# Two reorderings in a packed-attention and mixer kernel: bank by bank out of the fold, and a step ahead of w2's conversion

## The chip, the cores and the metric

The kernel runs on one core of one Trainium2 chip. The metric is the device time of one execution in microseconds (us); lower is better. The kernel before the change takes 829.05 us, the median of three runs (829.01 to 829.96 us).

The core's engines appear in the profile as PE (TensorE matmuls) and PEld (its weight loads), DVE (VectorE), ACT (ScalarE), POOL (GpSimd) and SP (SyncE, which here only issues DMAs). Each engine works through its own instructions in order and waits for the others at semaphores.

## What is computed

For eight batches, eight heads, 576 tokens and a head width of 64, with 32 packed rows `p` for each head:

```python
p_packed = softmax(scale * p @ k.T) @ v            # 32 rows for each head
out      = softmax(scale * q @ p_packed.T) @ p_packed
x  = out, heads side by side                       # 576 x 512 for each batch
u  = x + (x.T @ U @ V).T                           # rank 32 along the tokens
ch = relu(u @ w_ch1) @ w_ch2                       # 512 -> 2048 -> 512
result = u + ch
```

`U`, `V`, `w_ch1` and `w_ch2` arrive as 64-bit floats. The kernel takes them apart with integer operations on DVE ("conversion").

## The kernel before, in words

**Numbers.** Where more than one pass of precision is wanted a matrix is held as a high part and a low part; the product is then three matmuls (`mm3`, lines 85 to 89). A split is always the same pair: ACT copies the source into the high part with rounding, then DVE subtracts that from the source to get the low part.

**The fold.** The output of the second attention is never multiplied by `w_ch1` directly. For each batch `b` and each quarter `c` of `w_ch1`'s 2048 columns, `fold(b, c)` (lines 379 to 392) multiplies the packed rows of the eight heads by their part of `w_ch1`: sixteen small matmuls into two PSUM banks, `f_ps[0]` for heads 0 to 3 and `f_ps[1]` for heads 4 to 7. Each bank has 512 columns. They are emptied by four splits of 256 columns: an ACT copy into `wth` (line 390) and a DVE subtraction into `wtl` (line 391). The column half `a` chooses which pair of tiles is filled, the bank `g` which half of that pair. The two banks come from a pool `psT` of two (`bank()`, line 96), which all the small products of the attention use in turn.

**Before the loop.** Up to line 576 the first attention of all batches, the conversion of `w_ch1`, the second attention of batch 0 and `fold(0, 0)` are put in order by a planner, which simulates the program and picks what comes next on each engine.

**The large loop.** From line 579 on (`manual_schedule`) each engine runs its instructions in the order in which the program writes them. For each batch there are sixteen iterations `kt`, one for each 128 columns of the hidden layer:

- `gemm1(kt)`, the first product (lines 621 to 638): twelve matmuls into two banks `h_ps0` and `h_ps1`. ACT writes the rectified high part `hh` (line 634), and the rectified last 64 columns into `hj` (line 636); DVE makes the low part `hl` (line 637).
- a first place for a step of the next batch's attention (line 722);
- `gemm2(kt - 1)`, the second product (lines 640 to 648): twelve matmuls into the four output banks, with in batch 0 one more step between its halves;
- in iterations 2, 6, 10 and 14 a `fold`, which is used two iterations later; in iteration 6 also the 64 small matmuls of `add_u`;
- in batch 0 alone, the conversion of `w_ch2` by blocks of 128 rows (lines 738 to 746): `split_w2` of the block converted last (ACT copy of line 165, DVE subtraction of line 166), a DMA for a block to come (`load_w2`), and `convert_w2` of the next one (ACT at line 78, DVE at lines 79 to 82). Iteration 3 does this twice, iteration 8 not at all;
- a second place for a step (line 747), which iterations 2, 6, 10 and 14 do not have.

The steps of one batch's attention are listed at lines 349 to 374. Those named below: `turn_q(g, h)` transposes a piece of `q` on PE and copies it to `xT` with ACT (lines 229, 236, 239, 240); `scores_q` multiplies on PE into two banks (line 249), which DVE transposes into `e` (lines 283, 284); `softmax1` is a DVE maximum (line 289) and a POOL subtraction (line 290); `softmax2` an ACT exponential (line 293); `softmax3` a DVE sum and reciprocal (lines 298 to 300) and a POOL product; `tokens` turns back on PE and splits (lines 255 to 257, 319, 320); `mix2` is a product on PE (line 344), a DVE sum (345), an ACT copy (346) and a POOL subtraction (347), which gives `al`, an input of `gemm1`. A last group of steps, taken first in batch 0, ends the first attention: `a_heads` turns a packed result on PE (line 500) and copies it with ACT (line 501).

In batch 0 the second place of the iterations holds these steps: `turn_q(0, 2)` in 3, `softmax1(0)` in 4, `turn_q(1, 1)` with `softmax2(0)` in 5, `softmax3(1)` in 9, `tokens(0)` in 11 and `mix2(0, 0)` in 13; in the others nothing. Between the halves of the second product of iteration 4 stands the last `a_heads`.

Of the kernel before, what the change touches and what calls it, by code (L numbers as in the profile page):

```python
# [9 lines left out]
F32 = mybir.dt.float32  # L10
F32R = mybir.dt.float32r
I32 = mybir.dt.int32
AF = mybir.ActivationFunctionType
ALU = mybir.AluOpType
# [6 lines left out]
def packed_attention_mixer_kernel(  # L21
# [27 lines left out]
    nc = tc.nc  # L49
# [5 lines left out]
    P = 128  # L55
# [5 lines left out]
    QW = 512  # L61
# [30 lines left out]
    pipe = ctx.enter_context(tc.tile_pool(name="pipe", bufs=1))  # L92
# [3 lines left out]
    def bank():  # L96
        return psT.tile([P, 512], F32, name="t_ps", tag="t")
# [25 lines left out]
    def w2_tiles(pool, n):  # L123
        for i in range(n, n + 2):
            w2t[i] = tuple(pool.tile([P, 4, DM], F32R, name=f"w2{x}{i}", tag=f"w2{x}{i}", bufs=1) for x in "hl")
# [30 lines left out]
    def load_w2(kt):  # L156
        b = bits["w2", kt] = bits_tile()
        nc.sync.dma_start(out=b.rearrange("p x t -> p (x t)"), in_=w2[kt * P:(kt + 1) * P, :])

    def convert_w2(kt):  # L160
        return kt, float32_of(conv_tile(I32), conv_tile(F32), bits.pop(("w2", kt)))

    def split_w2(kt, x):
        hi, lo = w2_parts(kt)
        nc.scalar.copy(hi, x)
        (nc.gpsimd if kt == 0 else nc.vector).tensor_tensor(lo, x, hi.bitcast(F32), op=ALU.subtract)
# [210 lines left out]
    wt = {}  # L377

    def fold(b, c):
        f_ps = [bank() for _ in range(2)]  # L380
        for h in range(H):
            g, z = h // 4, h % 2
            xs, zs = slice(32 * (h % 4 ^ g), 32 * (h % 4 ^ g) + 32), slice(64 * z, 64 * z + 64)
            nc.tensor.matmul(f_ps[g][xs], lhsT=ppT[b][zs, g, xs], rhs=w1t[h // 2][zs, QW * c:QW * c + QW],  # L384
                             start=True, stop=True)
        for a in range(2):
            hi, lo = (pipe.tile([P, 2, QW // 2], F32R, name=f"wt{x}", tag=f"wt{x}", bufs=3) for x in "hl")
            cs = slice(QW // 2 * a, QW // 2 * a + QW // 2)
            for g in range(2):
                nc.scalar.copy(hi[:, g], f_ps[g][:, cs])  # L390
                nc.vector.tensor_tensor(lo[:, g], f_ps[g][:, cs], hi[:, g].bitcast(F32), op=ALU.subtract)  # L391
            wt[b, 2 * c + a] = hi, lo

    res = {}

# [137 lines left out]
    for i in range(NU):  # L533
# [26 lines left out]
        if i == 13:  # L560
            fold(0, 0)
        if i == 14:
            load_w2(0)
            load_w2(1)
            steps = attention(1, res)
# [28 lines left out]
    def get(b):  # L594
        aL[b] = sB.tile([32, H, I], F32, name="aL", bufs=2)
        ppP[b] = sB.tile([P, H, D], F32, name="ppP", bufs=2)
        a, y = (x.rearrange("(h n) x -> n h x", n=32) for x in (aD[b], ppD[b]))
        for t in range(4):
            ts_ = slice(32 * t, 32 * t + 32)
            nc.sync.dma_start(out=aP[ts_], in_=a[:, :, cols(t)])  # L600
            nc.sync.dma_start(out=ppP[b][ts_], in_=y)
        nc.sync.dma_start(out=aL[b], in_=a[:, :, LAST])
# [63 lines left out]
    def joint_parts(b, n):  # L666

        hi, lo = conv_tile(F32R), conv_tile(F32R)
        k0 = 4 * n
        for (dst, src) in ((slice(0, 1), jslot(b, k0)), (slice(1, 4), k0 + 1)):  # L670
            w = dst.stop - dst.start
            src = hj[:, src:src + w].rearrange("p k x -> p (k x)")
            cs = slice(P * dst.start, P * dst.stop)
            nc.scalar.copy(hi[:, cs], src)
            nc.vector.tensor_tensor(lo[:, cs], src, hi[:, cs].bitcast(F32), op=ALU.subtract)
        return hi, lo

    def joint(b, parts):

        oj = psO.tile([P, DM], F32, name="o", tag="o")  # L680
        for kt in range(NK):
            if kt % 4 == 0:
                hi, lo = parts.pop(0)
                if kt // 4 + 2 < NK // 4:
                    parts.append(joint_parts(b, kt // 4 + 2))
            cs = slice(P * (kt % 4), P * (kt % 4) + P)
            mm3(oj, (hi[:, cs], lo[:, cs]), w2_parts(kt), kt == 0, kt == NK - 1)
            if kt == 0:
                for h, i in product(range(H), range(2)):
                    nc.tensor.matmul(oj[I * i:I * i + I, place(h)], lhsT=aL[b - 1 + i][:, h], rhs=ppP[b - 1 + i][:32, h],  # L690
                                     start=False, stop=False)
        return oj

    def store_joint(b, oj):
        os_ = conv_tile(F32)
        n = DM // 2
        nc.scalar.copy(os_[:, :n], oj[:, :n])
        nc.vector.tensor_copy(os_[:, n:], oj[:, n:])
        for i, queue in enumerate((nc.sync, nc.scalar)):
            queue.dma_start(out=out[b - 1 + i].rearrange("(i c) m -> c i m", c=NT)[8], in_=os_[I * i:I * i + I])  # L700
# [10 lines left out]
    for b in range(B):  # L711
        cur = Batch(b)
        oj = None
        ahead = attention(b + 2, res) if b + 2 < B else []
        for kt in range(NK):
            cur.gemm1(kt)
            if b == 0 and kt < 2:
                w2x = convert_w2(n_w2)
                n_w2 += 1
            if oj and kt == 1:  # L720
                store_joint(b - 1, oj)
            if steps and (b < 2 or kt % 4 != 2) and (b, kt) != (1, 0):
                steps.pop(0)()
            if (b, kt) == (0, 5):
                w2_tiles(ctx.enter_context(tc.tile_pool(name="sC", bufs=1, side="right", reuse_waits="tile")), 2)
            if kt > 0:
                cur.gemm2(kt - 1, (rest or steps).pop(0) if b == 0 and (rest or steps) else None)
            elif last:
                last.gemm2(NK - 1)
                last.store()  # L730
                if last.b % 2 == 1:
                    oj = joint(last.b, parts)
            if kt % 4 == 2 and (b, kt) != (B - 1, NK - 2):
                n = b * NPC + kt // 4 + 1
                fold(n // NPC, n % NPC)
            if kt == 6:
                cur.add_u()
            for _ in range(pieces.get(kt, 1)):
                if w2x:
                    split_w2(*w2x)  # L740
                    w2x = None
                    if n_w2 + 1 < NK:
                        load_w2(n_w2 + 1)
                    if 0 < kt and n_w2 < NK:
                        w2x = convert_w2(n_w2)
                        n_w2 += 1
            if steps and kt % 4 != 2 and (b, kt) != (1, 0):
                steps.pop(0)()
            if kt == 1:
                get(b)  # L750
            if ahead and kt == (13 if b else NK - 1):
                ahead.pop(0)()
            if kt == NK - 1 and b % 2 == 1:
                parts = [joint_parts(b, 0), joint_parts(b, 1)]
        assert not steps
        steps = ahead
        last = cur
# [35 lines left out]
```

## Time and profile before

| | |
|---|---|
| time, median of three runs | 829.05 us |
| the three runs | 829.05, 829.01, 829.96 us |
| span of the profiled execution | 827.6 us |
| median less span | 1.4 us |
| PE busy | 799.1 us |
| PEld busy | 644.8 us |
| DVE busy | 364.6 us |
| ACT busy | 319.8 us |
| POOL busy | 81.3 us |

The profile is of one execution, from its first to its last instruction (the span). Its own time on the clock of the timed runs is not given; the median of these lies 1.4 us above the span, for what lies around the first and the last instruction. A timeline row gives the start, the duration, the engine, the line in the kernel, the operation with the tile that it writes and those that it reads, the shape, and how many instructions were merged into the row; in square brackets stands how long the engine was idle before it and what ended that. Matmul durations overlap: a following matmul starts before the one before it has ended. A window row gives for a stretch of time the busy time (and the number of instructions) of PE, PEld, DVE, ACT and POOL, the clock that TensorE was granted as a share of full speed, the DMA share and GB/s.

### The profile page before, as it was taken

To read this page: it belongs to the slowest core of one execution; us is meant where nothing else is said; L and a number is where in the kernel's file an instruction comes from. 1 tells how busy PE (TensorE), PEld (TensorE's weight loads), DVE (VectorE), ACT (ScalarE), POOL (GpSimd) and SP (SyncE) were. 2 spreads that over 40 slices of the span, in tenths; PEclk is the share of its full clock that TensorE was granted. 3 is DMA by queue.
4 is the path that set the end of the run, shared out by engine and by line. 5 is a ranking of instruction groups with operands and counts; after the bars stand their busy time and mean duration, and the time that the engine had idled before them with its cause. 6 is when DMAs were issued, how large, how long until landed. Compare 5 with 4: busy or idle time off the path is not lost.

```text
span 827.6 us, 15457 instructions
## 1 busy us (share of the span) xinstructions
PE 799.1 (97%) x6224; PEld 644.8 (78%) x6224; DVE 364.6 (44%) x815; ACT 319.8 (39%) x974; POOL 81.3 (10%) x115
## 2 busy tenths in 40 slices
PE   7788889999999999999999999999999999999997
PEld 5456567778888888888888888888888888887886
DVE  3789677783343333433334234333434234332232
ACT  5788764444223332333233232343234232332231
POOL 0222201100111001010101001010101011100000
PEclk8999999999999999999999999999999999999999
DMA  9999863216002220023002120122002200030001
GB/s 295 347 363 349 272 163 98 77 51 188 2 1 68 80 55 2 1 96 93 1 1 96 51 55 1 60 84 46 2 30 85 75 14 1 15 111 1 2 0 64
DMA packets 60310, 70.23 MB, mean 85 GB/s; under 512 B 22864, under 2 KB 41296, under 8 KB 60240
## 3 DMA queue, kind: packets, MB, share of 16 engines
q1 hardware_dynamic: 59920, 68.73, 26.6%
q8 instruction: 49, 0.80, 0.4%
q10 hardware_dynamic: 320, 0.52, 0.2%
q14 instruction: 21, 0.17, 0.1%
HBM read 53.64 MB, written 15.60 MB: 84 GB/s over the span
## 4 chain that ended last, share of the span: by engine, by line
PE 87%; DVE 5%; ACT 2%; DMA 1%; issue 1%; POOL 0%; ACTq 0%
PE o L87 16%; PE o L89 16%; PE o L88 16%; PE h_ps L87 9%; PE h_ps L89 8%; PE h_ps L88 8%; PE t_ps L384 4%; PE o L654 2%; PE t_ps L229 2%; PE t_ps L249 1%; DVE os L81 1%; PE t_ps L327 1%; PE t_ps L255 1%; DMA kx<-in_k_dram 1%; PE t_ps L344 1%
## 5 line engine op out<-in xcount | busy, mean ns | idle before, releaser
L87 PE MATMUL o<-w2h,hh 128*128 128x512 f32 x512 | 207.0, 404 | 0.0
L89 PE MATMUL o<-w2h,hl 128*128 128x512 f32 x512 | 202.9, 396 | 0.0
L88 PE MATMUL o<-w2l,hh 128*128 128x512 f32 x512 | 202.3, 395 | 0.0
L637 DVE SCALAR_TENSOR_TENSOR hl<-h_ps,hh 128x256 fp32r<-128x256 f32 x256 | 105.3, 423 | 203.3 <-ACT hj L636 189.3
L634 ACT ACTIVATE hh<-h_ps 128x256 fp32r<-128x256 f32 x256 | 98.8, 387 | 183.2 <-PE h_ps L89 182.5
L87 PE MATMUL h_ps<-ah,wth 128*128 128x320 f32 (+1 forms) x512 | 157.6, 308 | 0.8 <-DVE hl L637 0.8
L88 PE MATMUL h_ps<-al,wth 128*128 128x320 f32 (+1 forms) x512 | 151.5, 296 | 0.0
L89 PE MATMUL h_ps<-ah,wtl 128*128 128x320 f32 (+1 forms) x512 | 151.3, 296 | 0.0
L87 PEld LDWEIGHTS h_ps<-ah,wth 128*128 128x128 f32 x512 | 96.6, 189 | 26.2 <-issue 20.2
L89 PEld LDWEIGHTS o<-w2h,hl 128*128 128x128 f32 x512 | 96.6, 189 | 22.6
L87 PEld LDWEIGHTS o<-w2h,hh 128*128 128x128 f32 x512 | 97.3, 190 | 21.1 <-issue 4.6
L88 PEld LDWEIGHTS o<-w2l,hh 128*128 128x128 f32 x512 | 97.2, 190 | 16.8
L88 PEld LDWEIGHTS h_ps<-al,wth 128*128 128x128 f32 x512 | 96.8, 189 | 2.0
L89 PEld LDWEIGHTS h_ps<-ah,wtl 128*128 128x128 f32 x512 | 97.0, 189 | 0.0
L391 DVE TENSOR_TENSOR wtl<-t_ps,wth 128x256 fp32r<-128x256 f32 x128 | 48.5, 420 | 101.1 <-ACT wth L390 97.8
L390 ACT CAST wth<-t_ps 128x256 fp32r<-128x256 f32 x128 | 43.3, 374 | 109.3 <-PE t_ps L384 102.6
L347 POOL TENSOR_TENSOR al<-aT,ah 128x320 fp32r<-128x320 f32 (+1 forms) x32 | 25.7, 809 | 210.8 <-ACT ah L346 210.8
L290 POOL TENSOR_TENSOR e<-e,m 128x576 f32<-128x576 f32 x16 | 18.6, 1165 | 260.9 <-DVE m L289 259.1
L236 ACT COPY xT<-t_ps 128x256 f32<-128x256 f32 x64 | 21.3, 392 | 39.5 <-PE t_ps L229 38.8
L384 PE MATMUL t_ps<-w1t,ppT 64*32 64x512 f32 x512 | 34.9, 601 | 0.0
L346 ACT CAST ah<-aT 128x320 fp32r<-128x320 f32 (+1 forms) x32 | 13.8, 435 | 43.7 <-DVE aT L345 43.7
L636 ACT ACTIVATE hj<-h_ps 128x64 f32<-128x64 f32 x128 | 28.2, 220 | 0.0
(122 smaller groups left out, 838.3 us busy)
## 6 DMA issues: line engine op xcount, KB each, us to landing
bits<-in_moe_w_ch_dram SPq DMA_DIRECT2D x32, 512.0 KB, 6.2
kx<-in_k_dram SPq DMA_DIRECT2D x16, 576.0 KB, 7.2
x<-in_q_dram SPq DMA_DIRECT2D x16, 576.0 KB, 5.1
vt<-in_v_dram SPq DMA_DIRECT2D x32, 256.0 KB, 6.8
out_dram<-bits SPq DMA_DIRECT2D x32, 256.0 KB, 2.4
aD<-aT SPq DMA_DIRECT2D x16, 288.0 KB, 2.1
aP<-aD SPq DMA_DIRECT2D x32, 128.0 KB, 3.1
ppP<-ppD SPq DMA_DIRECT2D x32, 64.0 KB, 3.0
```

The source lines that it names most:

```text
L87: nc.tensor.matmul(ps, lhsT=lh, rhs=rh, start=start, stop=False)
L88: nc.tensor.matmul(ps, lhsT=lh, rhs=rl, start=False, stop=False)
L89: nc.tensor.matmul(ps, lhsT=ll, rhs=rh, start=False, stop=stop)
L236: nc.scalar.copy(dst, src[:, a])
L290: nc.gpsimd.tensor_tensor(e, e, m.unsqueeze(2).to_broadcast([P, S // 32, 32]), op=ALU.subtract)
L347: nc.gpsimd.tensor_tensor(al[:, g, ns], aT[:, ns], ah[:, g, ns].bitcast(F32), op=ALU.subtract)
L384: nc.tensor.matmul(f_ps[g][xs], lhsT=ppT[b][zs, g, xs], rhs=w1t[h // 2][zs, QW * c:QW * c + QW], start=True, stop=True)
L390: nc.scalar.copy(hi[:, g], f_ps[g][:, cs])
L391: nc.vector.tensor_tensor(lo[:, g], f_ps[g][:, cs], hi[:, g].bitcast(F32), op=ALU.subtract)
L634: nc.scalar.activation(hh[:, ms], src, AF.Relu)
L636: nc.scalar.activation(hj[:, jslot(self.b, kt), self.js], h_ps[:, LAST], AF.Relu)
L637: nc.vector.scalar_tensor_tensor(hl[:, ms], src, 0.0, hh[:, ms].bitcast(F32), op0=ALU.max, op1=ALU.subtract)
```

## The change

The change has two parts. In `fold` both pairs of tiles are taken from their pool first, and the four splits then run with the bank as the outer and the column half as the inner index: bank 0 left, bank 0 right, bank 1 left, bank 1 right, where before it was bank 0 left, bank 1 left, bank 0 right, bank 1 right. In the large loop the second step of an iteration is written ahead of `w_ch2`'s conversion instead of behind it. No instruction is added or removed, and PE's own order stays, since the conversion has no matmul in it.

```diff
@@ fold
         for a in range(2):
-            hi, lo = (pipe.tile([P, 2, QW // 2], F32R, name=f"wt{x}", tag=f"wt{x}", bufs=3) for x in "hl")
+            wt[b, 2 * c + a] = tuple(
+                pipe.tile([P, 2, QW // 2], F32R, name=f"wt{x}", tag=f"wt{x}", bufs=3) for x in "hl")
+        for g, a in product(range(2), range(2)):
+            hi, lo = (t[:, g] for t in wt[b, 2 * c + a])
             cs = slice(QW // 2 * a, QW // 2 * a + QW // 2)
-            for g in range(2):
-                nc.scalar.copy(hi[:, g], f_ps[g][:, cs])
-                nc.vector.tensor_tensor(lo[:, g], f_ps[g][:, cs], hi[:, g].bitcast(F32), op=ALU.subtract)
-            wt[b, 2 * c + a] = hi, lo
+            nc.scalar.copy(hi, f_ps[g][:, cs])
+            nc.vector.tensor_tensor(lo, f_ps[g][:, cs], hi.bitcast(F32), op=ALU.subtract)
@@ the large loop
             if kt == 6:
                 cur.add_u()
+            if steps and kt % 4 != 2 and (b, kt) != (1, 0):
+                steps.pop(0)()
             for _ in range(pieces.get(kt, 1)):
                 if w2x:
                     split_w2(*w2x)
...
                         w2x = convert_w2(n_w2)
                         n_w2 += 1
-            if steps and kt % 4 != 2 and (b, kt) != (1, 0):
-                steps.pop(0)()
             if kt == 1:
                 get(b)
```

## The prediction

> **What bounds the kernel now.** I read the span, then the busy time by stretches, to see where another engine than PE could set the pace.
>
> ```profile
> span 827.6 us, 15457 instructions
> 120.00:140.00 20.00, 17.40 (x114) 13.14 (x112) 14.93 (x31) 8.37 (x23) 1.88 (x2) 0.91 0.41 133
> 160.00:180.00 20.00, 19.32 (x124) 15.85 (x123) 17.80 (x36) 9.99 (x25) 1.09 (x3) 1.00 0.23 73
> 300.00:400.00 100.00, 99.82 (x689) 81.92 (x688) 36.82 (x86) 34.21 (x105) 9.60 (x11) 1.00 0.14 42
> ```
>
> From batch 2 on PE is busy without a hole (99.82 of 100 us), while DVE (36.82) and ACT (34.21) have room: there a later split costs nothing until PE needs its result. In batch 0 DVE is busy 14.93 and 17.80 of 20 us, for it converts w2 as well, and PE has holes (17.40 of 20). So the change is decided in batch 0, and in the few places where PE takes a bank soon after a fold.
>
> Next the timeline of one fold in the steady part, with the durations of its two lines.
>
> ```profile
> 428.45 0.65 ACT L390 CAST wth<-t_ps 128x256 fp32r<-128x256 f32 x2 [3.44 <-PE t_ps L384]
> 428.85 1.62 DVE L391 TENSOR_TENSOR wtl<-t_ps,wth 128x256 fp32r<-128x256 f32 x4 [3.38 <-ACT wth L390]
> 429.31 0.70 ACT L390 CAST wth<-t_ps 128x256 fp32r<-128x256 f32 x2 [0.22 <-DVE wtl L391]
> L390 ACT CAST wth<-t_ps x128: 363/373/384, 93.7 to 787.2; 128x256 fp32r<-128x256 f32 x128
> L391 DVE TENSOR_TENSOR wtl<-t_ps,wth x128: 414/422/426, 94.4 to 787.7; 128x256 fp32r<-128x256 f32 x128
> ```
>
> The third copy reads the same bank as the first subtraction, and other columns. It waits for that subtraction nevertheless (0.22 us, until DVE): ACT and DVE do not work in one bank at a time. While the banks alternate this hardly costs anything, since DVE meanwhile has the other bank.
>
> **Part 1: the fold.** Bank by bank, each second copy of a bank must wait for the subtraction before it. With 0.37 us for a copy, 0.42 for a subtraction and 0.03 for a hand-over (428.45 + 0.37 = 428.82, and DVE starts at 428.85): copy, subtraction, copy, subtraction end at 428.45 + 0.37 + 0.03 + 0.42 + 0.03 + 0.37 + 0.03 + 0.42 = 430.12. Before, the third subtraction freed bank 0; the four end at 428.85 + 1.62 = 430.47, the third one pitch earlier, at 430.14 (two DVE operations of 0.42 take 0.75 in the row of 166.80 below, so the pitch is 0.33). So bank 0 comes free no sooner. The third copy hides under the second subtraction, the third subtraction ends a pitch later, at 430.45, and the fourth copy and subtraction take 0.03 + 0.37 + 0.03 + 0.42 more: 431.3 in place of 430.47. Rounded upwards for the hand-overs, each fold ends 0.87 us later on both engines, and bank 1 comes free 0.87 later. Queued behind on ACT is the next `hh`, on DVE the next `hl`; from batch 2 on these are wanted an iteration later, so 0.87 is covered there. It is not covered in three places.
>
> ```profile
> 205.06 1.62 DVE L391 TENSOR_TENSOR wtl<-t_ps,wth 128x256 fp32r<-128x256 f32 x4 [3.57 <-ACT wth L390]
> 206.44 1.14 PE L249 MATMUL t_ps<-xT,ppT 64*32 64x320 f32 x16
> 188.61 1.44 POOL L347 TENSOR_TENSOR al<-aT,ah 128x256 fp32r<-128x256 f32 x2 [4.79 <-ACT ah L346]
> 190.58 0.28 PE L88 MATMUL h_ps<-al,wth 128*128 128x256 f32 x1
> 166.80 0.75 DVE L637 SCALAR_TENSOR_TENSOR hl<-h_ps,hh 128x256 fp32r<-128x256 f32 x2
> 167.27 0.42 PE L87 MATMUL h_ps<-ah,wth 128*128 128x320 f32 x1 [0.49 <-DVE hl L637]
> 171.17 0.41 PE L257 MATMUL t_ps<-ident,aT 128*64 128x128 f32 x2 [0.20 <-DVE x L320]
> ```
>
> In iteration 3 of batch 1 the scores use both banks at 206.44, while the last subtraction ends at 206.68: PE already waits within that row, so the whole 0.87 is added. At the start of batch 1 `al` is ready at 190.05 and used at 190.58; 0.87 less 0.53 of cover leaves 0.36 with the hand-over. In iteration 12 of batch 0 PE already waits for `hl` (0.49 us at 167.27), which follows the fold and a conversion on DVE: 0.87 is added in full. The 0.20 at 171.17 goes, because `tokens(0)` now precedes the conversion on DVE: 0.67 net.
>
> Before the loop the planner places one fold. Its order there cannot be read off. From below: bank 0 free one pitch earlier, perhaps 0.4 us of gain; from above: one fold's 0.87, with as much for neighbours that the planner moves. I take 0, the loop's start being set by other matmuls in front of it on PE.
>
> **Part 2: the step ahead of the conversion.** PE's order stays. What moves is the step's ACT, DVE and POOL work, past one ACT copy, one DVE subtraction, a w2 load on SP, one ACT pass and four DVE passes. None of the moved steps issues a DMA; the loads queue on SP as before and land an iteration ahead. The timeline of iterations 3 and 4 of batch 0:
>
> ```profile
> 118.38 0.63 ACT L165 CAST w2h<-os 128x512 fp32r<-128x512 f32 x1
> 119.05 0.69 DVE L166 TENSOR_TENSOR w2l<-os,w2h 128x512 fp32r<-128x512 f32 x1 [0.17 <-ACT w2h L165]
> 119.33 0.38 PE L239 MATMUL t_ps<-ident,x 128*64 128x128 f32 x2
> 122.02 0.62 ACT L165 CAST w2h<-os 128x512 fp32r<-128x512 f32 x1 [2.43 <-DVE os L82]
> 123.12 0.35 ACT L240 COPY xT<-t_ps 64x256 f32<-64x256 f32 x1
> 123.52 0.77 PE L249 MATMUL t_ps<-xT,ppT 64*32 64x320 f32 x16 [2.22 <-ACT xT L240]
> 126.20 0.51 DVE L283 STREAM_TRANSPOSE e<-t_ps 128x320 f32<-128x320 f32 x1
> 126.76 0.48 PE L500 MATMUL t_ps<-ident,two 128*128 128x128 f32 x1 [0.38 <-DVE e L283]
> 128.09 0.69 DVE L166 TENSOR_TENSOR w2l<-os,w2h 128x512 fp32r<-128x512 f32 x1 [1.05 <-ACT w2h L165]
> 125.00:126.00 1.00, 1.00 (x4) 0.52 (x2) 1.00 (x3) 0.00 (x0) 0.00 (x0) 0.57 0.00 0
> 128.00:129.00 1.00, 1.00 (x5) 0.82 (x4) 0.91 (x2) 0.64 (x2) 0.00 (x0) 0.72 0.40 131
> ```
>
> The visible stall is PE's 2.22 us before the scores: their `xT` copy stands behind two conversions. Moved ahead, it goes at once. But the next stall is not shortened: `a_heads` (126.76) waits for a bank that DVE's transposition frees, and DVE reaches that only after both conversions. And this chain now starts later. The `xT` copy needs transposes that PE ends at 119.33 + 0.38 = 119.71. In front of the conversion on ACT's queue, it holds back the copy of 118.38 until about 120.1 (119.75 plus its own 0.35): 1.7 us, which DVE passes on, since from 119.05 to 126.7 its only gap is that between two conversions. The fold's 0.87 of iteration 2 lies within these 1.7. So `a_heads` moves from 126.76 to 128.46: **+1.7**. The maximum of `softmax1` in iteration 4 then fits into DVE's 1.05 us of idle time before 128.09 and costs nothing.
>
> The holes merge, too. After the 2.22 us without matmuls the granted clock falls: the mean of 0.57 between 125 and 126 and of 0.72 between 128 and 129 put half speed from 125.14 to 128.56. Of these 3.4 us the part behind the wait, 126.76 to 128.56, cost 0.9. In the changed kernel PE idles from 124.2 at the latest (the work between the two waits took no more than 2.9 us) to 128.46, over 4 us. If one such stretch of 3.42 us then falls wholly on matmuls it costs 1.71, that is **+0.81**. By the Trainium skill ("TensorE: Matmul & The Clock Gate", Part 1: The HAM clock gate) half speed comes only after an idle window of about 3.4 us. The trace disagrees, since 2.22 us were enough; by either the longer hole is followed by half speed.
>
> Iteration 5 repeats the first pattern.
>
> ```profile
> 133.35 0.63 ACT L165 CAST w2h<-os 128x512 fp32r<-128x512 f32 x1
> 134.01 0.69 DVE L166 TENSOR_TENSOR w2l<-os,w2h 128x512 fp32r<-128x512 f32 x1 [1.66 <-ACT w2h L165]
> 134.59 0.67 ACT L236 COPY xT<-t_ps 128x256 f32<-128x256 f32 x2
> 135.14 0.70 ACT L293 ACTIVATE e<-e 128x576 f32<-128x576 f32 x1
> 135.72 0.38 ACT L634 ACTIVATE hh<-h_ps 128x256 fp32r<-128x256 f32 x1
> 136.27 0.69 DVE L82 SCALAR_TENSOR_TENSOR os<-bits,os 128x512 int32<-128x512 int32 x1
> 138.53 0.27 DVE L300 RECIPROCAL s<-s 128x18 f32<-128x18 f32 x1
> 140.60 1.62 DVE L391 TENSOR_TENSOR wtl<-t_ps,wth 128x256 fp32r<-128x256 f32 x4 [1.81 <-ACT wth L390]
> 150.31 0.75 DVE L637 SCALAR_TENSOR_TENSOR hl<-h_ps,hh 128x256 fp32r<-128x256 f32 x2
> 151.82 0.31 PE L87 MATMUL h_ps<-ah,wth 128*128 128x320 f32 x1
> ```
>
> The times that follow are on the clock of before, with PE's shift so far left out. The copies of 134.59 wait for PE's transposes in the middle of that iteration, and the exponential follows them; the w2 copy of 133.35 now starts when `hh` did, at 135.72, so DVE's chain starts 2.37 late. The idle time before 140.60 takes part of it back: the softmax sum ends at 138.80 + 2.37 = 141.17 instead of 138.80, the fold's first subtraction is 0.57 late rather than 2.37, and with the fold's 0.87 the lag is 1.44. From there DVE has no gap until 150.31. The first `hl` ends there at 150.73 + 1.44 = 152.17, while PE wants its bank at 151.82: **+0.38** with the hand-over. Behind it there are gaps, and the moved `softmax3` of iteration 9 fits into one.
>
> ```profile
> 178.40 0.30 PE L344 MATMUL t_ps<-vs,ms 128*128 128x320 f32 x1
> 181.88 0.49 DVE L345 TENSOR_TENSOR aT<-t_ps,aT 128x320 f32<-128x320 f32 x1
> 183.15 1.09 PE L384 MATMUL t_ps<-w1t,ppT 64*32 64x512 f32 x16
> ```
>
> In iteration 13 DVE's sum of `mix2` now stands ahead of the conversion and waits for PE's product (178.70). It ends at 179.22; the w2 copy follows one ACT slot later (0.37) at 179.6, DVE's chain 0.66 after it (as 134.01 after 133.35) at 180.3 and ends 2.95 later (134.01 to 136.96) at 183.2; two `hl` (0.75) and the next sum (0.49) end at 184.4. The fold's second half wants that bank half a fold after 183.15, at 183.65: **+0.75**.
>
> Sum: 1.7 + 0.81 + 0.38 + 0.67 + 0.75 + 0.36 + 0.87 = 5.5 us. The profiled span of 827.6 becomes 833.1; with the 1.45 by which the median of the runs lies above the span, **834.6 us**. The 2.22 us stall is not subtracted, since it lies ahead of a wait that ends later.
>
> **The rivals.** *Only the clock goes otherwise.* Half speed follows a hole in stretches of about 3.4 us, whose start need not fall on the same place. If it falls into the hole, the 1.71 are saved: 832.9. If a second stretch follows: 836.3. The rule named above, of windows that run free of the kernel, would give just this spread.
>
> *The lag is covered.* If PE needed neither `a_heads`' bank nor the later ones so soon, only the 0.87 in batch 1 would stay: 829.9. Against it: each wait is named in a row above, with PE as the waiter.
>
> *Faster.* The moved steps fill DVE's idle time (1.05 at 128.09, 1.66 at 134.01) and hold nothing up; the holes before the scores shrink, so the 0.9 of half speed goes, and DVE runs ahead far enough for the waits at 167.27 and 171.17 to go as well (0.49 and 0.20): 829.05 - 1.6 = 827.4, or 827.0 with the planner's 0.4. What decides is whether PE's transposes in iteration 3 are done when ACT is free for the conversion, at 118.38. They end at 119.71, 1.3 too late.
>
> *The loop's order is not the program's.* If something reordered ACT's queue by readiness, little would change: 829. But the rows show the `xT` copy waiting behind a conversion, in program order.
>
> **How the numbers follow.** Forecast 0.64, clock 0.15, covered or reordered 0.13, faster 0.08. The range goes from the covered case, 829.9, to a second stretch of half speed with a little for the planner, 837.0; below it lie about 0.1, above it about 0.05. A measurement of this kernel tells 0.2% from no change, 1.7 us. Slower than 830.7: the forecast, the clock and a rest of the others, 0.80; within: 0.12; faster: 0.08.
>
> **What would show it.** In the changed profile: the fold's four subtractions take 2.5 us instead of 1.62, with two waits on ACT; the scores in iteration 4 start without a wait at about 121.3 and `a_heads` waits 4 us or more for DVE, followed by half clock; w2's subtractions in iterations 3 and 5 start 1.7 and 2.4 us later against PE; waits of PE appear at the first product of iterations 9 and 12 and in the fold of iteration 14; from batch 2 on each iteration lasts as before. If `a_heads` starts no later than 126.8 my chain on DVE is wrong, and with it the sign.

## The result, and the profile after

The changed kernel takes 835.03 us (median of five runs, 834.45 to 835.72); the kernel before took 829.08 us beside it (five runs, 829.01 to 829.96). The ratio is 1.0069, with a 95% interval of 1.0057 to 1.0081: slower by 5.95 us, where 5.5 were forecast. The profiled execution took 834.45 us, 1.85 above its span.

Line numbers behind the fold are one higher than before: the fold's copy is line 392, its subtraction 393, `a_heads` 501, `hl` 638. The page, first the span, then the fold's two lines among the costliest groups (busy time and mean duration in ns, then the idle time before them):

```profile
span 832.6 us, 15459 instructions
L393 DVE TENSOR_TENSOR wtl<-t_ps,wth 128x256 fp32r<-128x256 f32 x128 | 51.3, 422 | 121.8 <-ACT wth L392 121.8
L392 ACT CAST wth<-t_ps 128x256 fp32r<-128x256 f32 x128 | 44.5, 374 | 132.9 <-PE t_ps L384 100.3
```

The copies and subtractions did not become longer: the means, 374 and 422 ns, lie within the 363 to 384 and 414 to 426 of before. What grew is the waiting between them. (The two instructions that the changed profile counts more are semaphore waits on DVE.) The busy time by stretches:

```profile
120.00:140.00 20.00, 15.21 (x89) 12.46 (x89) 13.84 (x25) 8.61 (x24) 1.16 (x1) 0.83 0.35 109
300.00:400.00 100.00, 99.82 (x699) 81.38 (x698) 37.27 (x85) 34.01 (x105) 9.59 (x11) 1.00 0.18 51
```

In the steady part PE is as full as before (99.82). In batch 0, between 120 and 140, it lost 2.2 of 20 us (15.21 against 17.40), and the granted clock is 0.83 in place of 0.91. The fold of the steady part, on ACT and DVE:

```profile
433.45 0.37 ACT L392 CAST wth<-t_ps 128x256 fp32r<-128x256 f32 x1 [3.44 <-PE t_ps L384]
433.86 0.42 DVE L393 TENSOR_TENSOR wtl<-t_ps,wth 128x256 fp32r<-128x256 f32 x1 [3.38 <-ACT wth L392]
434.31 0.65 ACT L392 CAST wth<-t_ps 128x256 fp32r<-128x256 f32 x2 [0.49 <-DVE wtl L393]
434.72 0.76 DVE L393 TENSOR_TENSOR wtl<-t_ps,wth 128x256 fp32r<-128x256 f32 x2 [0.44 <-ACT wth L392]
435.51 0.37 ACT L392 CAST wth<-t_ps 128x256 fp32r<-128x256 f32 x1 [0.55 <-DVE wtl L393]
435.91 0.43 DVE L393 TENSOR_TENSOR wtl<-t_ps,wth 128x256 fp32r<-128x256 f32 x1 [0.44 <-ACT wth L392]
```

The two engines take turns twice: ACT waits 0.49 and 0.55 us for DVE, DVE 0.44 twice for ACT. From the first copy to the last subtraction it is 436.34 - 433.45 = 2.89 us, before 430.47 - 428.45 = 2.02: 0.87 more, as worked out. Iterations 3 and 4 of batch 0:

```profile
119.16 0.36 ACT L240 COPY xT<-t_ps 64x256 f32<-64x256 f32 x1 [1.33 <-PE t_ps L239]
119.42 0.62 ACT L165 CAST w2h<-os 128x512 fp32r<-128x512 f32 x1
120.08 0.69 DVE L166 TENSOR_TENSOR w2l<-os,w2h 128x512 fp32r<-128x512 f32 x1 [1.08 <-ACT w2h L165]
120.64 0.76 PE L249 MATMUL t_ps<-xT,ppT 64*32 64x320 f32 x16
127.23 0.51 DVE L283 STREAM_TRANSPOSE e<-t_ps 128x320 f32<-128x320 f32 x1
127.79 0.47 PE L501 MATMUL t_ps<-ident,two 128*128 128x128 f32 x1 [4.79 <-DVE e L283]
128.94 1.16 POOL L290 TENSOR_TENSOR e<-e,m 128x576 f32<-128x576 f32 x1 [10.51 <-DVE m L289]
129.12 1.52 DVE L166 TENSOR_TENSOR w2l<-os,w2h 128x512 fp32r<-128x512 f32 x1 [0.26 <-ACT w2h L165]
```

The scores (120.64) start without a wait; the stall of 2.22 us in front of them is gone, as intended. But ACT now waits 1.33 us with the `xT` copy in hand, the `w2` copy stands behind it, and the next wait of PE, that of `a_heads` for DVE, is 4.79 us in place of 0.38. The clock in the same stretch (the seventh number is the granted share):

```profile
125.00:126.00 1.00, 0.00 (x0) 0.00 (x0) 0.93 (x3) 0.00 (x0) 0.00 (x0) 0.61 0.89 365
131.00:132.00 1.00, 1.00 (x6) 1.00 (x5) 0.95 (x2) 0.00 (x0) 0.00 (x0) 0.50 0.89 365
132.00:133.00 1.00, 1.00 (x9) 1.00 (x9) 0.89 (x3) 0.53 (x2) 0.00 (x0) 0.98 0.12 37
```

Half speed holds from 125.2 to 132.0, 6.8 us, twice as long as before; 4.2 us of it fall on matmuls. The other places that the prediction named, at the first product of iteration 12 and in the fold of iteration 14 of batch 0, and at the scores in iteration 3 of batch 1:

```profile
170.58 0.42 PE L87 MATMUL h_ps<-ah,wth 128*128 128x320 f32 x1 [1.35 <-DVE hl L638]
182.79 0.88 POOL L347 TENSOR_TENSOR al<-aT,ah 128x320 fp32r<-128x320 f32 x1 [21.75 <-ACT ah L346]
183.19 1.02 DVE L166 TENSOR_TENSOR w2l<-os,w2h 128x512 fp32r<-128x512 f32 x1 [1.05 <-ACT w2h L165]
186.07 1.06 PE L384 MATMUL t_ps<-w1t,ppT 64*32 64x512 f32 x8
187.04 0.48 DVE L345 TENSOR_TENSOR aT<-t_ps,aT 128x320 f32<-128x320 f32 x1
187.58 1.06 PE L384 MATMUL t_ps<-w1t,ppT 64*32 64x512 f32 x8 [0.45 <-DVE aT L345]
211.81 0.76 PE L249 MATMUL t_ps<-xT,ppT 64*32 64x256 f32 x14 [0.54 <-DVE wtl L393]
```

**Where the time came from.** I measure an iteration from the start of the first product of its `gemm1` to the start of the next iteration's, so that a wait at a first product counts to the iteration before it. The loop begins with these rows, in the kernel before and in the changed one:

```profile
98.33 0.41 PE L87 MATMUL h_ps<-ah,wth 128*128 128x320 f32 x1
```

```profile
97.59 0.41 PE L87 MATMUL h_ps<-ah,wth 128*128 128x320 f32 x1
```

From there to the end of the span it is 827.6 - 98.33 = 729.27 us before and 832.6 - 97.59 = 735.05 after (starts and spans here and below unrounded): **+5.78**. The beginning of the loop itself lies anywhere between 97.6 and 101.3 us in the profiles of this study, so below the loop is compared apart from the medians. Kernels with the same program ahead of the loop differ by up to 2 us there (the changed kernel 97.59, the one without the move in 5, below, 99.62). The two latest beginnings, 101.29 and 100.87, belong to the two kernels with the copies first, below; their profiled executions are also the slowest of their runs (828.17 with a median of 825.14, and 824.05 with 822.81), so one profile each does not tell whether the kernel or the execution was late.

| iteration | before, us | after, us | difference |
|---|---|---|---|
| batch 0: 3 / 4 / 5 | 6.43 / 9.66 / 5.18 | 6.58 / 11.75 / 5.81 | +0.15 / +2.09 / +0.63 |
| 8 / 9 | 4.41 / 4.39 | 4.65 / 4.48 | +0.24 / +0.08 |
| 11 / 12 | 5.56 / 5.55 | 6.43 / 5.16 | +0.87 / -0.38 |
| 14 / 15 | 5.63 / 5.05 | 7.12 / 4.71 | +1.48 / -0.34 |
| batch 1: 0 / 3 | 4.40 / 5.85 | 4.44 / 6.72 | +0.04 / +0.86 |
| batches 2 to 7 | | | 0 |

The iterations of batches 0 and 1 that are not listed differ by 0.02 us or less.

### The profile page after: what moved, and what is told of

Read it like the earlier page. It is cut to its first block, busy times and chain, and to the rows that moved or that the text cites. A ratio compares the mean times of both kernels' runs of the same rounds, so it can differ in the third digit from the quotient of the medians.

```text
span 832.6 us, 15459 instructions
## 1 busy us (share of the span) xinstructions
PE 802.4 (96%) x6224; PEld 647.0 (78%) x6224; DVE 369.0 (44%) x815; ACT 319.5 (38%) x974; POOL 81.2 (10%) x115
## 4 chain that ended last, share of the span: by engine, by line
PE 83%; DVE 6%; ACT 3%; DMA 3%; issue 1%; POOL 0%; SPq 0%; DVEq 0%
PE o L87 16%; PE o L89 15%; PE o L88 15%; PE h_ps L87 8%; PE h_ps L88 8%; PE h_ps L89 8%; PE t_ps L384 4%; DMA bits<-in_moe_w_ch_dram 2%; PE o L655 2%; PE t_ps L229 1%; DVE os L81 1%; PE t_ps L327 1%; PE t_ps L249 1%; PE t_ps L255 1%; DVE wtl L393 1%
## 5 line engine op out<-in xcount | busy, mean ns | idle before, releaser
L393 DVE TENSOR_TENSOR wtl<-t_ps,wth 128x256 fp32r<-128x256 f32 x128 | 51.3, 422 | 121.8 <-ACT wth L392 121.8
```

What stands on the lines that cost most here:

```text
L393: nc.vector.tensor_tensor(lo, f_ps[g][:, cs], hi.bitcast(F32), op=ALU.subtract)
```

## The experiments

The theory is the prediction's: the fold's turns within a bank cost 0.87 us wherever someone waits, and a step ahead of the conversion makes the conversion wait for that step's data. Its first rival was that the moved step helps and only the fold costs; its second, that the clock decides.

**Each part alone.** The first kernel has only the change to `fold`, the second only the step's move.

> Only the fold's order is changed; the step stays behind the conversion. My theory (ACT and DVE take turns in one bank, each fold ends 0.87 us later, and DVE in batch 0 passes that on): +0.8 at iteration 4 of batch 0 (the lag of the fold in iteration 2 goes through both conversions to the wait of the last turned head for its bank), +0.87 at the first product of iteration 12, up to 0.36 at the start of batch 1, +0.87 at the scores in iteration 3 of batch 1: 2.5 to 2.9 us above before, about 831.8. Rival (the fold's order counts only where PE takes both banks at once, in batch 1): +0.9, about 830.

> Only the step is moved ahead of the conversion; the fold stays as before. My theory (the moved step's ACT copy waits for PE and holds back the conversion behind it): the scores in iteration 4 start without a wait, the last turned head waits about 5 us for DVE, half clock follows: +2.7 over iterations 3 to 5; no wait at iteration 9 (the lag there is 0.57 against 1.1 of cover), 0.2 to 0.36 less at iteration 12, +1.1 in the fold of iteration 14: 3.2 to 3.7 us above before, about 832.5. Rival (the loss comes from the fold's waits and the moved step gains the 2.2 us of PE idle time before the scores): 827 to 829.

Measured: the fold alone 832.83 us (ratio 1.0045, 1.0031 to 1.0058), its loop +3.82; the step alone 833.30 us (1.0053, 1.0041 to 1.0065), its loop +3.99. Both are about 1 us slower than expected (831.8 and 832.5). The rival that the step is a gain falls. In the loop of the first, iteration 11 of batch 0 has +0.86 and iteration 3 of batch 1 +0.86, each one fold's lag; the start of batch 1 has +0.47 and iteration 4 +1.49, more than expected. The rows of the fold alone, iteration 4, and the stretch around it:

```profile
124.74 1.32 PE L249 MATMUL t_ps<-xT,ppT 64*32 64x320 f32 x16 [2.77 <-ACT xT L240]
128.71 0.41 PE L501 MATMUL t_ps<-ident,two 128*128 128x128 f32 x1
120.00:140.00 20.00, 17.23 (x98) 13.87 (x97) 15.24 (x31) 9.18 (x25) 1.16 (x1) 0.83 0.38 113
```

The hole before the scores grew only from 2.22 to 2.77 us, yet the mean clock fell from 0.91 to 0.83: here too half speed lasted two stretches (124.2 to 131.1), and most of it on matmuls (the scores took 1.32 us in place of 0.77). The step alone has +2.09 in iteration 4, +1.14 in 5, +1.48 in 14, -0.38 in 12 and -0.34 in 15. Iterations 8 and 9 change with neither part alone: the lag there needs both, as the prediction's 0.57 + 0.87 against 1.1 of cover has it. The parts add up to 7.8 and together give 5.78: the fold's lag of iteration 2 lies under ACT's wait in iteration 3, and the two do not pay twice for half speed. The start of `a_heads`, reckoned from the loop's first product, shows the first of these: the step alone puts it off by 1.59 us (28.43 to 30.02), the fold on top of that by 0.18 (30.20).

**Single steps put back.** Three kernels are the changed one with the step of one iteration behind the conversion again, 3, 13 or 5:

```diff
-            if steps and kt % 4 != 2 and (b, kt) != (1, 0):
+            if steps and kt % 4 != 2 and (b, kt) != (1, 0) and (b, kt) != (0, 3):
                 steps.pop(0)()
...
+            if (b, kt) == (0, 3):
+                steps.pop(0)()
```

> As the changed kernel, but in iteration 3 of batch 0 alone the step stands behind the conversion again. My theory: the conversion of block 4 starts early again, the last turned head waits about as long as before plus 0.8 from the fold of iteration 2, and the half-clock stretch covers less work: 2 to 2.2 us below the changed kernel, about 833. Rival (ACT's wait in iteration 3 is not the cause; DVE would be late anyway): no gain, or 2 us slower than the changed kernel, since PE's 2.2 us stall before the scores returns.

> As the changed kernel, but in iteration 13 of batch 0 alone the step stands behind the conversion again. My theory (DVE's sum of that step waits for PE, the conversion behind it is late, and the next step's bank is not free when the fold of iteration 14 wants it): iteration 14 falls from 7.12 to about 5.6 us and iteration 15 rises by 0.3; the others stay. Rival (the fold's order makes iteration 14 longer): 7.12 stays.

> As the changed kernel, but in iteration 5 of batch 0 alone the step stands behind the conversion again. My theory (the lag of DVE at iteration 9 starts with the w2 copy that waits behind PE's transposes in iteration 5): the 0.24 and 0.08 us that iterations 8 and 9 are longer than before go; the others stay. Rival (the lag comes from the fold of iteration 6 alone): they stay.

Without the move in 3: 832.57 us (1.0039, 1.0027 to 1.0051); the loop is 2.41 shorter than that of the changed kernel, iteration 4 has +0.35 instead of +2.09, and 5 nothing. The rows of that kernel:

```profile
124.16 0.77 PE L249 MATMUL t_ps<-xT,ppT 64*32 64x320 f32 x16 [2.76 <-ACT xT L240]
127.41 0.48 PE L501 MATMUL t_ps<-ident,two 128*128 128x128 f32 x1
```

The 2.76 us in front of the scores are back, the 4.79 at `a_heads` are gone, and the loop is 2.4 us faster with the visible stall than without it. The other two have one profiled run each, beside which the kernel before took 830.10 us. Without the move in 13 (834.39 us) iterations 14 and 15 are those of before again, and the start of batch 1 has the +0.47 that the fold alone showed. Without the move in 5 (836.26 us, its loop beginning at 99.62) the +0.24 and +0.08 of iterations 8 and 9 are gone and the other differences named stay. In both the half clock in iterations 4 and 5 fell a little otherwise (6.8 us from 126.6 and from 127.7, with +1.13 and +0.83 in iteration 5), so their totals say less than their iterations.

**The clock by itself.** The hole at `a_heads` was filled with 18 matmuls of a matrix of zeros, added to two output banks, so that no result changes. The first kernel uses a tile of its own for the zeros, the second 64 rows of zeros that the kernel holds anyway:

```diff
+                if t == 2 and self.b == 0 and kt == 3:
+                    nil = ua4[I:, 4].rearrange("p a r -> p (a r)")
+                    for n in range(18):
+                        nc.tensor.matmul(self.o[n % 2], lhsT=nil, rhs=w2_parts(kt)[0][I:], start=False, stop=False)
                 if t == 2 and between:
                     between()
```

> As the changed kernel, with 18 products of a block of zeros into two output banks (they add zero) between the halves of the second product of iteration 3's columns, just ahead of the last turned head: PE is busy through most of its 5 us wait there. My theory (the hole is what brings half clock, from 125.2 to 132.0 us, of which 4.2 us lie on work): the wait's end stays, set by DVE, the half clock goes and about 2.1 us with it: about 833. Rival (the low clock does not come from this hole, or zeros do not count as work): no change, 835.

> As the changed kernel, with the hole of iteration 4 filled again, this time without a tile of its own: 18 products over 64 rows whose weights are zeros that the kernel holds already. My theory (the hole brings half clock, and the filled kernel before lost its gain to something ahead of the loop): the loop from its first product to the end is 1.9 us shorter than in the changed kernel, the time about 833. Rival (the clock goes back for another reason, or half the rows are too little work): the loop is as long as in the changed kernel, 835.

The first one's rows, and its clock around them:

```profile
125.13 4.29 PE L650 MATMUL o<-w2h,nil 128*128 128x512 f32 x18
130.08 0.33 PE L501 MATMUL t_ps<-ident,two 128*128 128x128 f32 x1 [0.67 <-DVE e L283]
130.00:135.00 5.00, 4.92 (x30) 4.37 (x30) 4.75 (x8) 2.28 (x6) 1.16 (x1) 1.00 0.43 136
```

`a_heads` waits for the same DVE row as ever and starts no earlier, 30.21 and 30.24 us after the loop's first product against 30.20 in the changed kernel, but the clock stays at 1.00. The loops are 1.94 and 1.95 us shorter than that of the changed kernel, with iteration 4 at +0.79 and iteration 5 at 0. That is the price of half speed there, measured twice. In the medians the second gives 833.38 us (1.0055, 1.0042 to 1.0067), 1.65 below the changed kernel; the first 834.9 us (1.0062, 1.0050 to 1.0074), no gain that can be told. Its loop began at 99.86 in the profile; why what lies ahead of the loop took longer in it stays open.

**The turns, without the order of the banks.** If the turns cost and not the order, bank by bank must cost nothing once both copies of a bank go first and both subtractions follow. The loop is that of before.

```diff
+        for g in range(2):
+            parts = [(*(t[:, g] for t in wt[b, 2 * c + a]), f_ps[g][:, QW // 2 * a:QW // 2 * a + QW // 2])
+                     for a in range(2)]
+            for hi, lo, src in parts:
+                nc.scalar.copy(hi, src)
+            for hi, lo, src in parts:
+                nc.vector.tensor_tensor(lo, src, hi.bitcast(F32), op=ALU.subtract)
```

> Kernel before, with the fold's banks emptied in turn, but in each bank both ACT copies first and both DVE subtractions behind them, so that ACT never has to wait for DVE in a bank. My theory (the turns of ACT and DVE within one bank cost the 0.87 us of a fold, not the order of the banks): the four splits end about 2.1 us after the fold's products, as before (2.07), bank 0 comes free 0.3 us sooner; time as before, 829.1, within 0.7. Rival (emptying one bank after the other is what costs, since the second bank is started late): as the fold alone, 832.8.

Measured: **825.14 us** (0.9954, 0.9940 to 0.9968), faster than before by 3.9, where I expected no difference. The theory of the turns stands, for the banks are emptied in the order of the changed kernel; but my reading that nothing waited for bank 0 falls. The rows of this kernel, in iteration 11 of batch 3 as in the fence of the prediction:

```profile
428.13 1.09 PE L384 MATMUL t_ps<-w1t,ppT 64*32 64x512 f32 x16
429.26 1.20 ACT L393 CAST wth<-t_ps 128x256 fp32r<-128x256 f32 x4 [3.43 <-PE t_ps L384]
429.94 1.42 DVE L395 TENSOR_TENSOR wtl<-t_ps,wth 128x256 fp32r<-128x256 f32 x4 [3.66 <-ACT wth L393]
430.73 0.28 PE L89 MATMUL h_ps<-ah,wtl 128*128 128x256 f32 x1
430.85 0.62 PE L255 MATMUL t_ps<-ident,aT 128*128 128x128 f32 x4
```

and of the kernel before, at the same place:

```profile
429.92 0.28 PE L89 MATMUL h_ps<-ah,wtl 128*128 128x256 f32 x1
430.29 0.63 PE L255 MATMUL t_ps<-ident,aT 128*128 128x128 f32 x4
```

ACT's copies now run on one another (four in 1.20 us), and so do the subtractions (four in 1.42 in place of 1.62). The second subtraction ends 0.33 + 0.42 = 0.75 after DVE's start, at 430.69, 1.43 us after the first copy; before, bank 0 came free 1.69 after it. And PE had been waiting for it: from the last product of `gemm1` to the next step's first one it is 430.29 - 429.92 = 0.37 us before, and 430.85 - 430.73 = 0.12 here, which is the distance of the products before it (430.61 to 430.73) and so no wait. The matmul's own 0.28 covers most of that gap, so it left almost no idle time and no bracket in the row: 99.82 of 100 us of the window were busy. It recurs in iterations 11 and 15 of most batches (-0.26 and -0.25 each, e.g. 5.35 to 5.09 and 4.93 to 4.68), about 3.2 us in all, and -0.28 comes in iteration 3 of batch 0. The rest of this profile's gain, -0.82 in iteration 4, is the clock's: the hole in front of the scores is as long as before (2.23 us, from 124.00), but no half speed followed it here.

**The supply of w2.** In the kernel before iteration 3 converts two blocks and iteration 8 none; both stalls of iterations 3 and 4 stand behind that. One block in each, with nothing else changed:

```diff
-    pieces = {3: 2, 8: 0}
+    pieces = {}
```

> Kernel before, with one w2 block for each iteration, that is without the second conversion in iteration 3 and the pause in iteration 8; fold and step as before. My theory (in iterations 3 and 4 DVE's chain of two conversions is what both waits of PE go back to): the xT copy goes early, the scores start without a wait, the last turned head waits under 0.5 us, no half clock there: about 4 us less in iteration 4; up to 1.5 us given back at iterations 8 to 10, where DVE now has a conversion more: 825 to 827. Rival (DVE is short of time in all of batch 0 and the wait only moves): 829.

Measured: 825.74 us (0.9961, 0.9948 to 0.9973), and iteration 4 takes 5.46 us in place of 9.66. Its rows:

```profile
119.47 0.37 ACT L240 COPY xT<-t_ps 64x256 f32<-64x256 f32 x1 [0.17 <-PE t_ps L239]
120.96 0.76 PE L249 MATMUL t_ps<-xT,ppT 64*32 64x320 f32 x16
123.16 0.27 PE L500 MATMUL t_ps<-ident,two 128*128 128x128 f32 x1
```

Neither the scores nor `a_heads` wait, in the order of before. Of the 1.5 us that I allowed for iterations 8 to 10 nothing was given back there, only 0.12 in iteration 11. The stall that the step's move aimed at goes when the queue is made shorter, without a change of its order.

**What is left together.** Both copies first in the fold, one block of w2 an iteration, and the step ahead of the conversion only in iterations 4, 9 and 11 of batch 0, where nothing was found to wait for it:

```diff
+            early = steps and b == 0 and kt in (4, 9, 11)
+            if early:
+                steps.pop(0)()
```

> The three together: one w2 block for each iteration, the fold with both copies of a bank ahead of its subtractions, and the step ahead of the conversion in iterations 4, 9 and 11 of batch 0 only, where it does not make ACT or DVE wait for PE. My theory: as the even conversion, and 0.2 to 0.5 us less at iteration 12: 824.5 to 826.5. Rival (a step ahead of the conversion costs wherever it stands): not under the even conversion alone.

Measured: **822.81 us** (0.9925, 0.9912 to 0.9939), the fastest here. The loop is 7.87 us shorter than before: 4.20 in iteration 4, 0.38 in iteration 12, the rest mostly the 0.25 and 0.26 of bank 0 in iterations 15 and 11 of most batches. The expectation left that gain out.

## Why the prediction was right

**The fold's turns: right.** 0.87 predicted, 0.87 in the rows, and 0.86 to 0.87 where it was uncovered: at `hl` ahead of iteration 12 (the wait 1.35 against 0.49) and at the scores in iteration 3 of batch 1. The planner's part ahead of the loop: I took 0, and the loop of the profiled run begins 0.74 earlier, less than the 2 us by which its beginning differs between kernels with the same program there, so this term stays open.

**The wait of `a_heads`: right.** Reckoned from the loop's first product it moved from 126.76 - 98.33 = 28.43 us to 127.79 - 97.59 = 30.20: 1.77, where 1.7 was forecast (1.59 with the step alone). That the 2.22 us were not to be subtracted, since they lay ahead of a wait that ends later, is what the experiments on iteration 3 bear out from both sides.

**Half clock: right in kind, too small.** I forecast one stretch of 3.4 us wholly on matmuls, 1.71 against 0.9, so +0.81. There were two stretches, 4.2 us of them on matmuls, and filling the hole gave back 1.95. Against the 0.9 of before that is +1.05. Iterations 3 to 5 together: 2.87 for 2.51. The first rival priced a second stretch at 1.71 more; here 2.6 of the 6.8 us fell into the hole (125.2 to 127.8). The Trainium skill ("TensorE: Matmul & The Clock Gate", Part 1: The HAM clock gate) says of the windows after which the clock changes that they run free of the kernel. The runs agree: in the changed kernel, the step alone and the kernels without the move in 13 or in 5 the hole begins 25.2 to 25.4 us after the loop's first product and lasts 4.8, but half speed sets in 2.2, 3.4, 3.3 and 2.6 us after its beginning. So the size of this term is in part luck of the execution.

**Iterations 8 and 9: right.** +0.32 for 0.38, and gone with the move in 5 or with either part alone. **Iterations 11 and 12: +0.49 for 0.67**, since the step ahead in 11 gave back 0.38 in iteration 12, not only the wait of 0.20 that I had seen.

**The fold of iteration 14: too small, +1.14 for 0.75.** The step that failed is "the fold's second half wants that bank half a fold after 183.15". The sixteen products do not run half after half: unstalled, all end within 1.09 us, stalled, eight alone take 1.06. So the other bank's products had run beside them; a row gives each as 64*32, a full product as 128*128. Bank 1 is therefore wanted as soon as the fold begins, and a late bank costs a second pass: from 186.07 to 187.58 + 1.06 = 188.64 it is 2.57 us for 1.09, which is the +1.48 of iteration 14. Besides, DVE's `w2` subtraction at 183.19 took 1.02 us for 0.69. The -0.34 in iteration 15 goes the other way: bank 0, filled by the first pass, was emptied meanwhile, and most of the wait for it that the experiment on the copies laid bare fell away. From the last product of `gemm1` to that of `mix2` it is 0.37 us in the kernel before, 0.12 in the changed one, and 0.37 again with the move in 13 undone; that is 0.25 of the 0.34.

**The start of batch 1: wrong in this kernel, 0.04 for 0.36.** The fold's lag does reach `al`: alone it costs 0.47 there, and again 0.47 with the move in 13 undone. In the changed kernel PE's stall in iteration 14 came first and covered it. I had added two terms of which the one hides the other.

**The steady part: half right.** "There a later split costs nothing" holds: batches 2 to 7 did not move. But I took the full window for the absence of a wait. Bank 0 was late by a quarter of a microsecond at two steps of most batches, in the kernel before and after alike, and the order of the splits within a bank decides that.

So the total, 5.78 in the loop for 5.5, is close partly because two terms that were too small (1.05 for 0.81, 1.14 for 0.75) stand against the 0.36 that did not appear and the 0.18 too much in iterations 11 and 12. That these nearly cancel is luck.

## What to carry to other kernels

When two engines may not work in one PSUM bank at a time, let the first finish with a bank before the second begins: copy, copy, subtract, subtract, not copy, subtract twice (825.14 against 832.83 us here, with the banks in the same order). Before a step is moved ahead of other work on an engine, find when its data are ready: a step that still waits at the head of a queue delays everything behind it, and a removed stall counts only if no later wait ends at the same point. And a window that shows an engine busy all the time can still hide waits shorter than one instruction's duration; compare start to start with a place that has no wait.

## What the runs showed of the hardware

**Half clock.** Holes of 2.2 us (before) to 4.8 us were followed by half speed in stretches of 3.4 or 6.8 us, and a hole of 2.77 us got 6.8 in one profile (the fold alone), one of 2.76 us 3.4 in another (without the move in 3), one of 2.23 us none in a third (copies first): the length of the hole does not tell the length of the stretch. What does tell it in these runs is where the hole lies. In each profile the clock changes at times that are whole multiples of 3.413 us apart (before: 67.12 to 125.15 is 17 of them, 125.15 to 128.56 one). In batches 0 and 1 of all twelve profiles, a window of this grid at full clock in which PE idled 1.78 to 3.39 us was followed by half speed (seven windows), one with 1.39 us or less never; at half clock, up to 0.38 us of idle time was followed by full speed, 0.52 to 2.58 by another window at half. Ahead of the loop windows with 1.55 to 1.73 us idle went both ways, and at half clock those with 0.23 to 0.38, so idle time is not the whole measure; no run was made to test it. The hole of 2.77 us reached 0.52 us into the second window, that of 2.76 us ended before it, and that of 2.23 us was divided, so that its windows had 1.39 and 1.07 us. Matmuls with zeros as weights kept the clock at 1.00, on all 128 rows and on 64 alike.

**POOL beside DVE.** The moved steps bring POOL's work beside the conversion, and DVE operations whose tensors all lie in SBUF can grow longer there: the `w2` subtraction took 1.52 us in place of 0.69 beside the POOL subtraction of 128.94, and 1.02 beside that of 182.79. In the kernel before none of its fifteen was longer than 0.694, and none ran beside POOL. It is not always DVE's that grows: in the changed kernel the subtraction of 158.33 began 0.23 us ahead of POOL's product of 158.56 and took 0.63, while the product took 1.41 in place of 1.16, and the next DVE pass, that of line 79 with one input, 1.38 in place of 0.42. In these four the later one grew by what was left of the earlier one, less about 0.14 us: 0.83 with 0.98 left, 0.33 with 0.48, 0.25 with 0.40, 0.96 with 1.09. So it looks as if the later one waited for the earlier to end. Operations that read PSUM did not suffer: `hl` of the kernel before, two in 0.74 us from 131.61, ran beside a POOL subtraction from 131.78. The Trainium skill ("GPSIMD Engine Reference", 1. Specifications) says that GpSimd contends for SBUF with DVE instructions that have two SBUF inputs or run in a 2-port mode. The rows of the `w2` subtraction, which has two, agree; no row tells the mode of the pass with one input, and no experiment here takes POOL's part away alone.
